# Pooled attention and a feed-forward layer on one core: the first batch times v and the first run in float32 whole, and two pieces for batches 5 to 7

## The chip, the cores and the metric

One core of a Trainium2 chip runs one program. The metric is the device time of one execution in microseconds (us). The kernel before takes 1009.37 us (median of 3 runs, 1008.57 to 1009.87).

## The reference

```python
k_p = k.reshape(B, H, Sp, 8, D).mean(axis=3)      # q, k, v: 8 x 8 x 576 x 64, Sp = 72
v_p = v.reshape(B, H, Sp, 8, D).mean(axis=3)
scores = np.matmul(q, k_p.transpose(0, 1, 3, 2)) / 8
attn = softmax(scores)                             # over the 72 pooled keys
x = heads_side_by_side(np.matmul(attn, v_p))       # 4608 tokens x 512
h = x @ w_in                                       # 512 x 2048
out = np.maximum(0.01 * h, h) @ w_out              # 2048 x 512
```

All inputs and the output are float32.

## The kernel before

**Numbers.** A float32 value that goes into a large matmul is kept as two tiles of the packed type float32r, its rounded value (hi) and the rest (lo). A product is then three matmuls: hi with hi, hi with lo, lo with hi. Splitting a tile costs a cast on ACT and a subtraction on DVE. The scores and all transposes run on float32 as it is; in the trace a float32 matmul is two records.

**Attention.** Keys and values are pooled by POOL (batch 0 in part by DVE). place_k and place_v lay them out: kT by transposes on PE, v_hi and v_lo by a scaled copy on ACT and a subtraction on DVE (L342, L343); the eight keys past 64 go into v_rem through matmuls (pv, L357). A batch has 576 tokens, which PIECES cuts into pieces of one to three tiles. Per tile and group of four heads stand: q transposed (q_unit, pq L369, copied to qT by ACT, L371), scores (s_unit, pss L394, row maximum on DVE, four exponentials e on ACT, L404), division (norm_unit, at, on POOL or DVE, L418), and the transpose of the result (p_unit, pp L443, cast to pT_hi and pT_rem on ACT, pT_lo and pT_rem by DVE, L445 to L453). Per piece and group av_unit makes two accumulators pa of four matmuls each (L468 to L471, at least 256 columns wide except in batch 0), and these are split into x's hi and lo (xh L479, xl L480); tokens past 512 of batches 0 and 1 wait in x_tail (L482).

**Feed-forward.** The 4608 tokens are nine chunks of 512. A part is one chunk with one of 16 blocks f of 128 hidden units: m1 (12 matmuls into ph, L651 to L653), Prelu on ACT (L656), split into gh and gl (L659, L660), and m2 (12 matmuls into four accumulators acc, L675 to L677) two parts later. The table runs orders them: run 0, the first run, is chunk 0 with f 0 to 7; run 1 is chunk 1 whole; run 2 is chunk 0 with f 8 to 15, added to what run 0 left in DRAM (partial); then chunks 2 to 8. A run ends with store (acc copied to o by ACT and DVE, L697, L698, then a DMA).

**Weights.** stage loads them as raw bits; a head (head in convert) turns them into float32 w_t with two activations on ACT (L184, L185) and three operations on DVE (L186, L187, L190), and a tail splits them into w (cast on ACT L194, subtraction on DVE L195). There are 32 of each, spread by convert_to over FIRST (the steps "c"), run 0 and run 1. A head's ACT steps may not be issued ahead of the third last cast of gh (after, with BEHIND). w_t and o share three buffers.

**Order.** PE's order is that in which the code is written. FIRST lists batch 0's units; behind its "/" only two PSUM banks are left for attention, so a transpose or score waits until the bank of two groups back is emptied. Beside each run the attention units of a later chunk are laid between the halves of m1 and m2 by line_up: batch 0's last tile and batch 1 beside run 0, batch 2 on from run 2. The order on ACT, DVE, POOL and SP is found by a scheduler.

## Time and profile before

| | |
|---|---|
| profiled execution | 1009.92 us, of which the span is 1008.1 |
| mean granted clock of PE | 0.978 |
| PE busy | 960.3 us (95%), 4584 instructions |
| PE's weight loads (PEld) | 785.7 us (78%) |
| ACT busy | 427.4 us (42%), 1386 instructions |
| DVE busy | 366.3 us (36%), 890 instructions |
| POOL busy | 177.7 us (18%), 292 instructions |
| DMA | 57.44 MB, mean 57 GB/s |
| chain that ended last | PE 89%, DVE 4%, ACT 3% |
| waits of PE from 59.9 to 134 us | 11.4 us |

Times are of one execution, in us from the start of its span. Matmuls follow each other faster than one lasts (about .23 us from start to start for 512 columns, with a shown duration of .39), so PE's pace is read from the starts. A wait is put down to what ended last before it. Rows of the waits give the total, the times, and the longest; rows of a timeline give start, duration, engine, line, operation and, in brackets, the idle time before and what ended it.

### The profile page before, as it was taken

The numbers are of one execution on the slowest core, as the hardware profiler recorded it, in microseconds if no ns is written. First come the engines' busy times: TensorE is split into PE (matmuls) and PEld (weight loads), VectorE is DVE, ScalarE is ACT, GpSimd is POOL, SyncE is SP. The second block draws the span as 40 slices with busy tenths as digits, with TensorE's granted clock in tenths as the row PEclk, the third lists the DMA queues.
The fourth block names the chain that finished last, engine by engine and source line by source line (L and its number), as shares of the span: only waits on it lengthen the run. The fifth ranks groups of instructions, "written<-read, shape, count | busy, mean of one in ns | idle before, by whom it ended". The sixth has DMA issues, their size and how long they took to land.

```text
span 1008.1 us, 12812 instructions
## 1 busy us (share of the span) xinstructions
PE 960.3 (95%) x4584; PEld 785.7 (78%) x4584; DVE 366.3 (36%) x890; ACT 427.4 (42%) x1386; POOL 177.7 (18%) x292
## 2 busy tenths in 40 slices
PE   4569999999999999999999999999999999999998
PEld 4457778888887878878888788888887788888886
DVE  5998639223333222232222323232322322231111
ACT  4778657234433333434343425333434334332221
POOL 3602200501036510141013301031100001000000
PEclk8689999999999999999999999999999999999999
DMA  9954311302034301130012202020200020001001
GB/s 241 279 172 133 101 46 44 112 23 69 1 107 115 91 8 44 32 92 12 20 44 58 58 11 63 3 61 1 63 11 11 1 63 1 1 1 42 1 1 42
DMA packets 65006, 57.44 MB, mean 57 GB/s; under 512 B 39856, under 2 KB 48048, under 8 KB 64944
## 3 DMA queue, kind: packets, MB, share of 16 engines
q1 hardware_dynamic: 64944, 56.64, 19.8%
q8 instruction: 36, 0.59, 0.2%
q14 instruction: 26, 0.21, 0.1%
HBM read 46.14 MB, written 10.49 MB: 56 GB/s over the span
## 4 chain that ended last, share of the span: by engine, by line
PE 89%; DVE 4%; ACT 3%; issue 1%; DMA 1%; SPq 0%; POOL 0%; DVEq 0%; ACTq 0%; POOLq 0%
PE ph L651 13%; PE acc L675 13%; PE ph L653 13%; PE ph L652 13%; PE acc L677 13%; PE acc L676 13%; PE pss L394 4%; PE pp L443 2%; PE pq L369 2%; ACT e L404 2%; PE pa L468 1%; PE pa L469 1%; PE pa L471 1%; PE pa L470 1%; DVE w_t L187 1%
## 5 line engine op out<-in xcount | busy, mean ns | idle before, releaser
L651 PE MATMUL ph<-xh,w 128*128 128x512 f32 x576 | 236.2, 410 | 0.0
L675 PE MATMUL acc<-w,gh 128*128 128x512 f32 x576 | 234.7, 408 | 0.0
L653 PE MATMUL ph<-xh,w 128*128 128x512 f32 x576 | 227.2, 394 | 0.0
L652 PE MATMUL ph<-xl,w 128*128 128x512 f32 x576 | 227.0, 394 | 0.0
L677 PE MATMUL acc<-w,gl 128*128 128x512 f32 x576 | 225.7, 392 | 0.0
L676 PE MATMUL acc<-w,gh 128*128 128x512 f32 x576 | 225.5, 392 | 0.0
L656 ACT ACTIVATE ph<-ph 128x512 f32<-128x512 f32 x144 | 84.2, 585 | 275.6 <-PE ph L653 275.4
L660 DVE TENSOR_TENSOR gl<-ph,gh 128x512 fp32r<-128x512 f32 x144 | 99.4, 691 | 264.9 <-ACT gh L659 264.0
L418 POOL TENSOR_TENSOR at<-e,red 128x256 f32<-128x256 f32 (+1 forms) x76 | 47.3, 622 | 561.8 <-DVE red L416 428.0
L404 ACT ACTIVATE e<-pss,red 128x72 f32<-128x72 f32 (+1 forms) x320 | 98.0, 321 | 108.8 <-DVE red L402 107.3
L653 PEld LDWEIGHTS ph<-xh,w 128*128 128x128 f32 x576 | 109.3, 190 | 24.4
L677 PEld LDWEIGHTS acc<-w,gl 128*128 128x128 f32 x576 | 108.4, 188 | 24.1
L651 PEld LDWEIGHTS ph<-xh,w 128*128 128x128 f32 x576 | 109.4, 190 | 22.2 <-issue 1.4
L675 PEld LDWEIGHTS acc<-w,gh 128*128 128x128 f32 x576 | 108.4, 188 | 21.9 <-issue 1.9
L652 PEld LDWEIGHTS ph<-xl,w 128*128 128x128 f32 x576 | 109.6, 190 | 19.4
L676 PEld LDWEIGHTS acc<-w,gh 128*128 128x128 f32 x576 | 108.6, 189 | 19.2
L659 ACT CAST gh<-ph 128x512 fp32r<-128x512 f32 x144 | 85.2, 592 | 3.1
L402 DVE TENSOR_REDUCE red<-pss 128x4 f32<-128x288 f32 (+1 forms) x80 | 36.1, 454 | 99.6 <-PE pss L394 98.5
L404 ACT ACTIVATION_READ_ACCUMULATOR e<-pss,red 128x1 f32 (+1 forms) x320 | 65.8, 206 | 0.0
L394 PEld LDWEIGHTS pss<-kT,qT 128*128 128x128 f32 (+1 forms) x320 | 49.4, 192 | 14.7 <-ACT qT L371 5.0
L394 PE MATMUL pss<-kT,qT 128*128 128x144 f32 (+1 forms) x320 | 55.9, 303 | 4.2 <-ACT qT L371 4.2
L449 DVE TENSOR_TENSOR pT_lo<-pp,pT_hi 128x256 fp32r<-128x256 f32 (+1 forms) x80 | 31.6, 395 | 69.5 <-ACT pT_rem L446 68.7
(90 smaller groups left out, 857.3 us busy)
## 6 DMA issues: line engine op xcount, KB each, us to landing
out_dram<-o SPq DMA_DIRECT2D x35, 256.0 KB, 2.1
q<-in_q_dram SPq DMA_DIRECT2D x32, 256.0 KB, 4.2
w_bits<-in_moe_w_in_dram SPq DMA_DIRECT2D x16, 512.0 KB, 3.6
w_bits<-in_moe_w_out_dram SPq DMA_DIRECT2D x16, 512.0 KB, 3.4
k0raw<-in_k_dram SPq DMA_DIRECT2D x16, 256.0 KB, 3.7
k1raw<-in_k_dram SPq DMA_DIRECT2D x16, 256.0 KB, 4.4
v0raw<-in_v_dram SPq DMA_DIRECT2D x16, 256.0 KB, 4.2
v1raw<-in_v_dram SPq DMA_DIRECT2D x16, 256.0 KB, 5.4
```

The lines of the kernel that those rows point to most:

```text
L394: nc.tensor.matmul(sc[:n, 2 * SP * i : 2 * SP * (i + 1)], qT[:, p, :n], kT[:, p, :, :].rearrange("d i s -> d (i s)"), start=True, stop=True,)
L404: ins = nc.scalar.activation(e[:n, h, :], scv[:n, h, :], AF.Exp, bias=mx[:n, h : h + 1], accum_out=sm[:n, h : h + 1],)
L418: eng.tensor_tensor(at[:n, 0:2, :].rearrange("a i (h s) -> a (i h) s", h=2), e[:n, :, 0:MAIN], sm[:n].unsqueeze(2).broadcast_to([n, 4, MAI ...
L651: nc.tensor.matmul(ph, w[:, 0, ks], xh[kk], start=kk == 0, stop=False)
L652: nc.tensor.matmul(ph, w[:, 0, ks], xl[kk], start=False, stop=False)
L653: nc.tensor.matmul(ph, w[:, 1, ks], xh[kk], start=False, stop=kk == NK - 1)
L656: nc.scalar.activation(ph, ph, AF.Prelu, alpha=0.01)
L659: casts.append(nc.scalar.copy(gh, ph))
L660: nc.vector.tensor_tensor(gl, ph, gh.bitcast(F32), op=ALU.subtract)
L675: nc.tensor.matmul(a, gh[:, r], hi, start=first, stop=False)
L676: nc.tensor.matmul(a, gh[:, r], lo, start=False, stop=False)
L677: nc.tensor.matmul(a, gl[:, r], hi, start=False, stop=last)
```

## The change

**Batch 0 times v.** For batch 0, v goes whole into v_first, pT's first two thirds are copied whole to a float32 tile and the rest is scaled on DVE; p·v is two float32 matmuls for an accumulator and not four packed ones (L498, L499 in the changed kernel). v_lo, pT_lo and a cast go.

**The first run.** Batch 0's 512 tokens are kept whole in whole_x (two copies on ACT, two on DVE for a piece; no split). The weights of f 0 to 7 stay as float32 in whole_w. m1 and m2 of run 0 are four float32 matmuls each (L710, L750), Prelu writes g directly (L716), and there is no gh and gl. The splits that runs 1 and 2 need come later: split(f - 3) at part f of run 0, f 5 to 7 in run 1, and chunk 0's x by split_first at f 3 of run 1. Heads are ordered so that w_in is a block ahead of w_out (lagged); their ACT steps, and the casts of the splits, may not be issued ahead of the last activation of m1 that is written before them (paced). FIRST has 3 steps "c" instead of 14, and stage(f + SPARE) is called by the head and not the tail.

**Batches 5 to 7.** They are cut like batches 1 and 4, into 256 and 320 tokens, where there were three pieces each. A piece may now cross the end of a chunk: what is past it is copied by DVE to x_tail or to a tile "over", and carry(c) splits it on ACT and DVE at the start of run c; for c = 2 it takes the place of tails, which stood at the end of run 2.

Lines of the changed kernel stand some 20 to 80 further on: head's ACT steps L206, L207, its DVE steps L208, L209, L212, the split L220, L221, transposes of p L468, xh L520, o L774.

**Moves.** ACT, from the last x copies of batch 0 to the first scores of its last tile, ahead of part 0. Before:

```order
L194 CAST w_1_438<-w_t_439 128x512
L348 ACTIVATE vremparts_829<-vremsum_161 64x64
L479 CAST xh_0_402<-pa_1_0_525 128x256
L479 CAST xh_1_403<-pa_1_1_532 128x256
L194 CAST w_1_493<-w_t_494 128x512
L479 CAST xh_2_404<-pa_1_2_539 128x256
L479 CAST xh_3_405<-pa_1_3_546 128x256
L371 COPY qT_4_564<-pq_4_559 128x4x64
```

And now, where vsum and vremsum are POOL's sums of batch 1:

```order
L517 COPY whole_x_375<-pa_1_0_456 128x256
L369 ACTIVATE v_hi<-vsum_162 64x4x64 x2
L375 ACTIVATE vremparts_696<-vremsum_163 64x64
L517 COPY whole_x_376<-pa_1_2_464 128x256
L398 COPY qT_4_477<-pq_4_472 128x4x64
L431 ACTIVATE e_4_0_493,red_4_0_494<-pss_4_0_490,red_4_0_494 64x72 x4
```

The two casts of weights are gone, and batch 1's v_hi and vremparts stand ahead of the last copy of x.

ACT in part 4 of run 0, around the first x of batch 1. Before:

```order
L404 ACTIVATE e_2_0_983,red_2_0_984<-pss_2_0_980,red_2_0_984 128x72 x4
L656 ACTIVATE ph_4_973<-ph_4_973 128x512
L479 CAST xh_0_1006<-pa_0_0_1001 128x256
L659 CAST gh_4_997<-ph_4_973 128x512
L184 ACTIVATE w_bits_862<-w_bits_862 128x512
L185 ACTIVATE w_bits_862<-w_bits_862 128x512
L479 CAST xh_1_1007<-pa_0_1_1016 128x256
```

And now:

```order
L716 ACTIVATE g_4_839<-ph_4_824 128x512
L206 ACTIVATE w_bits_643<-w_bits_643 128x512
L207 ACTIVATE w_bits_643<-w_bits_643 128x512
L206 ACTIVATE w_bits_595<-w_bits_595 128x512
L207 ACTIVATE w_bits_595<-w_bits_595 128x512
L220 CAST w_2_917<-whole_538 128x512
L220 CAST w_2_920<-whole_538 128x512
L520 CAST xh_0_846<-pa_0_0_841 128x256
L520 CAST xh_1_847<-pa_0_1_856 128x256
```

xh_0 stood directly behind the activation; now two heads and two casts are between.

ACT at the start of run 1, where the first run's accumulators are copied to o. Before:

```order
L656 ACTIVATE ph_1_1438<-ph_1_1438 128x512
L659 CAST gh_1_1452<-ph_1_1438 128x512
L697 COPY o_0_1459<-acc_0_807 128x256
L184 ACTIVATE w_bits_1276<-w_bits_1276 128x512
L185 ACTIVATE w_bits_1276<-w_bits_1276 128x512
L184 ACTIVATE w_bits_1425<-w_bits_1425 128x512
L185 ACTIVATE w_bits_1425<-w_bits_1425 128x512
L697 COPY o_1_1466<-acc_1_811 128x256
L697 COPY o_2_1473<-acc_2_840 128x256
L697 COPY o_3_1480<-acc_3_844 128x256
L656 ACTIVATE ph_2_1504<-ph_2_1504 128x512
```

And now:

```order
L729 ACTIVATE ph_2_1300<-ph_2_1300 128x512
L732 CAST gh_2_1314<-ph_2_1300 128x512
L206 ACTIVATE w_bits_1085<-w_bits_1085 128x512
L774 COPY o_2_1269<-acc_2_707 128x256
L207 ACTIVATE w_bits_1085<-w_bits_1085 128x512
L206 ACTIVATE w_bits_997<-w_bits_997 128x512
L207 ACTIVATE w_bits_997<-w_bits_997 128x512
L549 CAST xh_0_1353<-whole_x_375 128x512
L549 CAST xh_1_1354<-whole_x_375 128x512
L549 CAST xh_2_1355<-whole_x_376 128x512
L549 CAST xh_3_1356<-whole_x_376 128x512
L774 COPY o_3_1274<-acc_3_709 128x256
```

o_2 and o_3 stood ahead of part 2's activation; now they stand behind it, o_3 also behind the four casts of chunk 0's x.

The diff, cut to its core:

```diff
         WHOLE,
-        [[(0, 128), (128, 64)], [(192, 128), (320, 128)], [(448, 128)]],
-        [[(0, 128)], [(128, 128), (256, 128)], [(384, 128), (512, 64)]],
-        [[(0, 64)], [(64, 128), (192, 128)], [(320, 128), (448, 128)]],
+        WHOLE, WHOLE, WHOLE,
...
     FIRST = (
...
-        "c q4 c c / sa40 sa41 sb40 sb41 c c c"
+        "q4 c / sa40 sa41 sb40 sb41"
...
+    WHOLE_W = {0: (1, 0), 1: (2, 0), 2: (3, 0), 3: (6, 0), 4: (6, 1), 5: (7, 0), 6: (7, 1)}
+    whole_w = {}
+    def whole_weights(f):
+        if f not in whole_w:
+            shape, name = [P, 2, DM], f"whole{f}"
+            whole_w[f] = (
+                spare(*WHOLE_W[f], shape, F32, name) if f in WHOLE_W
+                else two.tile(shape, F32, tag="raw", name=name)
+            )
+        return whole_w[f]
+    def paced():
+        after = casts[-1] if casts else anchor.get("act")
+        return tc.issue_after(after.ins) if after else nullcontext()
...
             low, high = b[:, :, 0], b[:, :, 1]
-            ws[i, f] = spare(f, i, [P, 2, DM], F32R, f"w{i}_{f}")
-            t = five.tile([P, DM], I32, tag="o", name=f"w{i}_t{f}")
-            st["w"] = t.bitcast(F32)
-            after = casts[-BEHIND] if len(casts) >= BEHIND else anchor.get("act")
-            with tc.issue_after(after.ins) if after else nullcontext():
+            if f < SPLIT:
+                t = whole_weights(f)[:, i, :]
+                st["w"] = t
+                t = t.bitcast(I32)
+            else:
+                t = five.tile([P, DM], I32, tag="o", name=f"w{i}_t{f}")
+                st["w"] = t.bitcast(F32)
+            with paced():
...
+        def tail():
+            w, t = spare(f, i, [P, 2, DM], F32R, f"w{i}_{f}"), st["w"]
+            ws[i, f] = w
+            with paced() if f < SPLIT else nullcontext():
+                nc.scalar.copy(w[:, 0, :], t)
+            nc.vector.tensor_tensor(w[:, 1, :], t, w[:, 0, :].bitcast(F32), op=ALU.subtract)
...
             r = slice(64 * i, 64 * i + 64)
+            if b == 0:
+                nc.scalar.mul(v_first[r, :, i, :], sums[r], 1.0 / POOL)
+                continue
...
         rem = pc["rem"][:, o : o + n]
+        if b == 0:
+            anchor["act"] = nc.scalar.copy(pc["hi"][:, :, o : o + n], pp[:, 0:2, :n])
+            nc.vector.tensor_scalar_mul(rem, pp[:, 2, :n], m_lo)
+            return
         nc.scalar.copy(pc["hi"][:, :, o : o + n], pp[:, 0:2, :n])
-        ins = nc.scalar.copy(rem, pp[:, 2, :n])
-        if b == 0:
-            anchor["act"] = ins
+        nc.scalar.copy(rem, pp[:, 2, :n])
...
             vr = v_rem[:, g, 2 * i : 2 * i + 2, :].rearrange("a i d -> a (i d)")
-            nc.tensor.matmul(pa, vh, pc["hi"][:, i, :w], start=True, stop=False)
-            nc.tensor.matmul(pa, vh, pc["lo"][:, i, :w], start=False, stop=False)
-            nc.tensor.matmul(pa, vl, pc["hi"][:, i, :w], start=False, stop=False)
-            nc.tensor.matmul(pa, vr, pc["rem"][:, :w], start=False, stop=True)
+            if b == 0:
+                vw = v_first[:, p, :, :].rearrange("a i d -> a (i d)")
+                nc.tensor.matmul(pa, vw, pc["hi"][:, i, :w], start=True, stop=False)
+                nc.tensor.matmul(pa, vr.bitcast(F32), pc["rem"][:, :w], start=False, stop=True)
+            else:
+                nc.tensor.matmul(pa, vh, pc["hi"][:, i, :w], start=True, stop=False)
+                nc.tensor.matmul(pa, vh, pc["lo"][:, i, :w], start=False, stop=False)
+                nc.tensor.matmul(pa, vl, pc["hi"][:, i, :w], start=False, stop=False)
+                nc.tensor.matmul(pa, vr, pc["rem"][:, :w], start=False, stop=True)
...
                 c, o = divmod(2 * TAIL + S * (b - 2) + s0, CH)
-                c, m = c + 2, n
-            if m:
+                c, m = c + 2, min(n, CH - o)
+                if m < n and c + 1 not in waiting:
+                    to = x_tail
+                    if n - m > 2 * TAIL:
+                        to = two.tile([P, NK, POOL * D // 2], F32, tag="raw", name=f"over{c}")
+                    waiting[c + 1] = to, n - m
+            if m and c == 0:
+                (nc.vector.tensor_copy if i else nc.scalar.copy)(whole_x(p)[:, o : o + m], pa[:, :m])
+            elif m:
...
             if m < n:
-                nc.vector.tensor_copy(x_tail[:, p, TAIL * b : TAIL * (b + 1)], pa[:, m:n])
+                to, o = (x_tail, TAIL * b) if b < 2 else (waiting[c + 1][0], 0)
+                nc.vector.tensor_copy(to[:, p, o : o + n - m], pa[:, m:n])
...
+    whole_xs = []
+    def whole_x(kk):
+        if not whole_xs:
+            whole_xs.extend(spare(11, i, [P, 2, CH], F32, f"whole_x{i}") for i in range(2))
+        return whole_xs[kk // 2][:, kk % 2, :]
+    def split_first():
+        for kk, (h, l) in enumerate(zip(*x_parts(0))):
+            with paced():
+                nc.scalar.copy(h, whole_x(kk))
+            nc.vector.tensor_tensor(l, whole_x(kk), h.bitcast(F32), op=ALU.subtract)
+    waiting = {2: (x_tail, 2 * TAIL)}
+    def carry(c):
+        held, n = waiting[c]
+        for kk, (h, l) in enumerate(zip(*x_parts(c))):
+            w = held[:, kk, :n]
+            nc.scalar.copy(h[:, :n], w)
+            nc.vector.tensor_tensor(l[:, :n], w, h[:, :n].bitcast(F32), op=ALU.subtract)
...
         n, c, f = parts[k]
+        nm = f"{c}_{f}"
+        ph = ps_h.tile([P, CH], F32, tag="h", name=f"ph{nm}")
+        if n == 0:
+            for kk in range(NK):
+                ks = slice(kk * P, (kk + 1) * P)
+                nc.tensor.matmul(
+                    ph, whole_w[f][:, 0, ks], whole_x(kk), start=kk == 0, stop=kk == NK - 1
+                )
+                if kk == 1:
+                    yield
+            g = three.tile([P, CH], F32, tag="gh", name=f"g{nm}")
+            casts.append(nc.scalar.activation(g, ph, AF.Prelu, alpha=0.01))
+            gs[k] = g, None
+            yield
+            return
...
         w = ws[0, f]
-        nm = f"{c}_{f}"
-        ph = ps_h.tile([P, CH], F32, tag="h", name=f"ph{nm}")
...
         gh, gl = gs.pop(k)
-        hi, lo = ws[1, f][:, 0, :], ws[1, f][:, 1, :]
+        if n > 0:
+            hi, lo = ws[1, f][:, 0, :], ws[1, f][:, 1, :]
...
             a = accs[t]
-            nc.tensor.matmul(a, gh[:, r], hi, start=first, stop=False)
-            nc.tensor.matmul(a, gh[:, r], lo, start=False, stop=False)
-            nc.tensor.matmul(a, gl[:, r], hi, start=False, stop=last)
+            if n == 0:
+                nc.tensor.matmul(a, gh[:, r], whole_w[f][:, 1, :], start=first, stop=last)
+            else:
+                nc.tensor.matmul(a, gh[:, r], hi, start=first, stop=False)
+                nc.tensor.matmul(a, gh[:, r], lo, start=False, stop=False)
+                nc.tensor.matmul(a, gl[:, r], hi, start=False, stop=last)
...
-    for i, f in [(i, f) for f in range(NF) for i in range(2)]:
+    def lagged(lo, hi):
+        fs = [(0, f) for f in range(lo, hi)], [(1, f) for f in range(lo, hi)]
+        out = [fs[0].pop(0)]
+        while fs[1]:
+            out += [side.pop(0) for side in fs if side]
+        return out
+    steps, splits, last = [], {}, None
+    for i, f in lagged(0, SPLIT):
+        head, splits[i, f] = convert(i, f)
+        steps.append(head)
+    for i, f in lagged(SPLIT, NF):
         head, tail = convert(i, f)
-        steps.append(head)
-        if last:
-            steps.append(last)
+        steps += [head, last] if last else [head]
...
+    def split(f):
+        for i in range(2):
+            if (i, f) in splits:
+                splits.pop((i, f))()
...
         us = list(units[n])
+        if n >= 2 and n in waiting:
+            us.insert(0, lambda n=n: carry(n))
...
             if n == 0:
-                convert_to(14 + 2.8 * f)
+                convert_to(3 + 2 * (f + 1) + max(0, f - 5))
+                split(f - 3)
             elif n == 1:
-                convert_to(36 + 3 * f)
+                split(f + SPLIT - 3)
+                convert_to(2 * SPLIT + 4 + 3 * (f + 1))
+                if f == 3:
+                    split_first()
```

More of the change, by code (lines that the diff above doesn't have):

```diff
@@ L60, in tile_pooled_attention_ffn @@
         WHOLE,
[3 rows of a table removed]
+        WHOLE, WHOLE, WHOLE,
     ]
     FIRST = (
[3 rows of a table removed]
+        "lk ku q0 q1 sa00 sb00 sa01 sb01 lv sa10 sb10 sa11 sb11 q2 sa20 sa21 vu pu00 pu10 sb20 q3 "
+        "pu01 pu11 sb21 au00 sa30 sa31 c au01 pu20 pu21 sb30 sb31 c pu30 pu31 au10 au11 "
+        "q4 c / sa40 sa41 sb40 sb41"
     )
@@ L120, in tile_pooled_attention_ffn @@
     nc.gpsimd.memset(kT, 0.0)
+    nc.gpsimd.memset(v_first, 0.0)
     nc.gpsimd.memset(v_hi.bitcast(F32), 0.0)
@@ L190, in head @@
             nc.vector.tensor_tensor(t, t, low, op=ALU.add)
-        def tail():
-            w, t = ws[i, f], st["w"]
-            nc.scalar.copy(w[:, 0, :], t)
-            nc.vector.tensor_tensor(w[:, 1, :], t, w[:, 0, :].bitcast(F32), op=ALU.subtract)
             if i == 1:
                 stage(f + SPARE)
+        def tail():
[4 more added lines that the diff above has]
+            nc.vector.tensor_tensor(w[:, 1, :], t, w[:, 0, :].bitcast(F32), op=ALU.subtract)
         return head, tail
@@ L372, in q_unit @@
         return qT
-    WIDE = {("at", 1): (8, 0), ("at", 2): (8, 1), ("at", 3): (7, 0),
-            ("e", 1): (7, 1), ("e", 2): (6, 0), ("e", 3): (6, 1)}
+    WIDE = {("at", 1): (0, 0), ("at", 2): (0, 1), ("at", 3): (1, 1),
+            ("e", 1): (2, 1), ("e", 2): (3, 1), ("e", 3): (8, 0)}
     wides = {}
@@ L431, in piece_tiles @@
     def piece_tiles(b, j, g):
-        if b > 0 or g == 0 or j == 2:
+        if b > 0:
             return pT
-        return {
-            part: spare(10 - n // 2, n % 2, t.shape, F32R, f"pT_{part}{b}_{j}_{g}")
-            for n, (part, t) in enumerate(pT.items())
-        }
+        t = spare(10 - j % 2, g, [P, 3, PMAX], F32, f"pT{b}_{j}_{g}")
+        return {"hi": t[:, 0:2, :], "rem": t[:, 2, :]}
     def p_unit(b, t, g, at, pc, o):
@@ L494, in x_parts @@
         return xs[c]
-    def tails():
-        for kk, (h, l) in enumerate(zip(*x_parts(2))):
-            h, l = h[:, : 2 * TAIL], l[:, : 2 * TAIL]
-            nc.scalar.copy(h, x_tail[:, kk, :])
-            nc.vector.tensor_tensor(l, x_tail[:, kk, :], h.bitcast(F32), op=ALU.subtract)
+    whole_xs = []
[15 more added lines that the diff above has]
+            nc.vector.tensor_tensor(l[:, :n], w, h[:, :n].bitcast(F32), op=ALU.subtract)
     q_of = {}
@@ L708, in store @@
             nc.sync.dma_start(out[r : r + P, :], o)
-    steps = []
-    last = None
-    for i, f in [(i, f) for f in range(NF) for i in range(2)]:
+    def lagged(lo, hi):
[9 more added lines that the diff above has]
+    for i, f in lagged(SPLIT, NF):
         head, tail = convert(i, f)
-        steps.append(head)
-        if last:
-            steps.append(last)
+        steps += [head, last] if last else [head]
         last = tail
@@ L762, in tile_pooled_attention_ffn @@
         if n == 2:
-            us = [fetch] + us + [tails]
+            us = [fetch] + us
         units.append(us)
```

2 lines of the change are left out of this document (1 added, 1 removed), and 2 rows, old and new, of the table FIRST.

## Prediction

> **What bounds the kernel now.** I read the page's slices first, then the windows of the opening stages, the waits of PE from 59.9 us until run 1, and last the timelines of PE, ACT and DVE at single places. The sum is made against the profiled execution (1009.92 us: a span of 1008.1 and 1.8 around it); the median of the runs shown is 1009.37, so .55 comes off at the end. The 40 slices of 25.2 us, in tenths:
>
> ```profile
> PE   4569999999999999999999999999999999999998
> PEclk8689999999999999999999999999999999999999
> ```
>
> From the sixth slice on PE is full, at full clock; time is lost in the first five. Later the kernel gets shorter only through fewer PE columns, or longer through a new wait. The windows: PE, PEld, DVE, ACT and POOL busy (with counts), granted clock, DMA share, GB/s:
>
> ```profile
> 40.00:50.00 10.00, 5.69 (x23) 4.67 (x24) 10.00 (x26) 6.97 (x19) 3.69 (x7) 0.50 0.92 293
> 60.00:134.00 74.00, 62.58 (x308) 49.70 (x307) 54.34 (x134) 55.40 (x176) 11.36 (x20) 0.93 0.39 116
> 112.00:114.00 2.00, 2.00 (x5) 1.53 (x5) 1.08 (x3) 0.81 (x2) 0.75 (x2) 0.50 0.68 245
> 210.00:220.00 10.00, 10.00 (x46) 8.29 (x45) 2.07 (x6) 3.33 (x8) 0.00 (x0) 1.00 0.01 2
> ```
>
> Before the first run DVE is the bound (10.00 of 10). Beside it nobody is: DVE 73%, ACT 75%, PE 85%, and PE's clock is .93. There single waits decide. Steady runs (210 to 220) have ACT and DVE free two thirds of the time. PE's waits from 59.9 to 134 (total, times, longest):
>
> ```profile
> PE pp L443 <- DVE x_tail L482: 3.1, 2, 1.8
> PE pq L369 <- ACT e L404: 2.6, 2, 2.1
> PE pq L369 <- DVE kT L330: 2.4, 1, 2.4
> PE pa L469 <- DVE pT_lo L449: 0.9, 1, 0.9
> ```
>
> These make 9.0; seven smaller rows bring it to 11.4. Nearly all are one kind: the next transposes or scores wait for their PSUM bank (two are left after the "/") to be emptied by ACT or DVE, which have weight work queued ahead.
>
> **The change, part by part.** PE's timeline at the places that I use (start, duration, idle before):
>
> ```profile
> 51.94 0.50 PE L651 MATMUL ph<-xh,w 128*128 128x512 f32 x1
> 56.52 0.72 PE L443 MATMUL pp<-ident,at 64*128 64x64 f32 x3 [2.92 <-POOL at L418]
> 59.90 0.26 PE L468 MATMUL pa<-pT_hi,v_hi 128*128 128x64 f32 x1
> 111.21 0.57 PE L369 MATMUL pq<-ident,q 64*128 64x64 f32 x4 [2.08 <-ACT e L404]
> 133.94 0.39 PE L651 MATMUL ph<-xh,w 128*128 128x512 f32 x1
> ...
> 61.40 0.28 PE L468 MATMUL pa<-pT_hi,v_hi 128*128 128x64 f32 x1
> 61.52 0.28 PE L469 MATMUL pa<-pT_lo,v_hi 128*128 128x64 f32 x1
> ```
>
> Part 0 runs from 51.94 to 59.90; run 1 begins at 133.94.
>
> *The start.* Eleven weight steps and batch 0's splits leave ACT and DVE ahead of part 0. What is late next is POOL, with batch 1's v sums, since ACT's v_hi and vremparts of batch 1 now stand ahead of its last whole_x copy (the first order excerpt). POOL's last sums, and ACT's two steps as they ran elsewhere:
>
> ```profile
> 42.60 0.63 POOL L235 TENSOR_TENSOR vsum<-v1raw 128x128 f32<-128x128 f32 x1
> 43.20 0.49 POOL L235 TENSOR_TENSOR vremsum<-vremraw 64x64 f32<-64x64 f32 x1
> ...
> 20.17 0.90 ACT L342 ACTIVATE v_hi<-vsum 64x256 fp32r<-64x256 f32 x2
> 47.70 0.25 ACT L348 ACTIVATE vremparts<-vremsum 64x64 fp32r<-64x64 f32 x1
> ```
>
> vsum is there at 43.2; .9 for v_hi, .25 for vremparts, some .3 for the copy: 44.7, then qT_4 and scores: part 0 begins at about 45 if POOL keeps its times. It takes 3.4 us of float32 matmuls (below) and 2 of units and hops, since the 2.92 us wait for POOL at 56.52 has gone by then (batch 0's last pieces are normalized while PE waits for x). So part 0 ends at 50.4 and not 59.90: **-9.5**. If POOL stays behind, 4 of these are lost.
>
> *Float32 in the first run.* Prices, from scores (two float32 matmuls of 144 columns, four records) beside packed matmuls:
>
> ```profile
> 89.20 0.65 PE L394 MATMUL pss<-kT,qT 128*128 128x144 f32 x4
> 89.59 0.49 PE L675 MATMUL acc<-w,gh 128*128 128x512 f32 x1
> 89.92 0.39 PE L676 MATMUL acc<-w,gh 128*128 128x512 f32 x1
> 90.15 0.39 PE L677 MATMUL acc<-w,gl 128*128 128x512 f32 x1
> ...
> 100.76 0.28 PE L468 MATMUL pa<-pT_hi,v_hi 128*128 128x256 f32 x1
> 101.71 0.39 PE L651 MATMUL ph<-xh,w 128*128 128x512 f32 x1
> ...
> 124.93 0.31 PE L468 MATMUL pa<-pT_hi,v_hi 128*128 128x320 f32 x1
> 126.10 0.39 PE L675 MATMUL acc<-w,gh 128*128 128x512 f32 x1
> ```
>
> A packed 512 column matmul lasts .227 (89.92 to 90.15, rounded). The scores hold PE for .39, and the next packed matmul then stands .10 longer than .23 (89.59 to 89.92): .49 for 288 columns, or .87 for 512 in proportion, .85 with a fixed start taken off; I take .857. A half part (m1 or m2) is 4 x .857 = 3.43 instead of 12 x .227 = 2.72: +.71. Thirteen half parts lie between part 0 and run 1: **+9.2**. If the .10 is not the scores' own but a price of the change of format, a matmul costs .39/288 x 512 = .69, a half part 2.77, and the term is +.7; the .10 would then also go at most of the 42 changes in this stage (4.2 us). I lean to the first reading, and take half of the 4.2 back: **-2.1**. The two m2 of the first run that fall into run 1: **+1.4**. The 64 token piece of batch 0: 16 matmuls of .12 (61.40 to 61.52) become 8 at about the same: **-.9**.
>
> *The first run's waits.* ACT's and DVE's weight work, from their timelines:
>
> ```profile
> 61.62 0.69 ACT L184 ACTIVATE w_bits<-w_bits 128x512 f32<-128x512 f32 x1
> 63.83 0.61 ACT L194 CAST w<-w_t 128x512 fp32r<-128x512 f32 x1
> 64.34 0.27 ACT L445 CAST pT_hi<-pp 128x128 fp32r<-128x128 f32 x1
> ...
> 59.50 0.69 DVE L187 SCALAR_TENSOR_TENSOR w_t<-w_bits,w_t 128x512 int32<-128x512 int32 x1
> 60.10 0.69 DVE L195 TENSOR_TENSOR w<-w_t,w 128x512 fp32r<-128x512 f32 x1
> ```
>
> Two heads take ACT 2.2 us (61.62 to 63.83), a cast .51, a long DVE step .6. The change takes an activation's second pass and gl away, but sets two heads directly behind each activation, and from part 3 on two casts and two subtractions (second excerpt). In part 4, xh_0 stands behind g_4, two heads and two casts: .5 + 2.2 + 1.0. xl_0 stands behind DVE's six head steps and two subtractions (4.3) that begin 1.1 after the activation's input: 5.4, + .4 for itself, + .2 to reach PE. Until then pp_0_1 has no bank; PE has .9 of p·v to do: 5.1, and .2 for the hand-over between the two heads: 5.3. In part 1 to 2, kT stands behind four head activations on ACT and five head steps on DVE, and pq_0 waits for its bank: 3.9, where the 2.4 now was. By the same count: pq_4 behind e_3_0 2.7, batch 0's last p·v 1.05, pv behind v_rem and the two subtractions 1.6 and 1.0, the end of the run 1.7, one of .3. Together 17.5 against 11.4: **+6.2**. Bounds: half of today's (5.7), if the heads always find a gap; 20, if the hops add up.
>
> *The clock.* A clock of .93 over 74 us is 5.2 us lost. The 2.08 us wait at 111.21 is followed by 112 to 114 at .50 (1 us lost, .3 or more outside the window). Three waits longer than that, at some 1.5 each, make 4.5: **-.7**. The Trainium skill ("TensorE: Matmul & The Clock Gate", "Part 1: The HAM clock gate") states that the clock is halved after an idle window of about 3.4 us. By that rule pq_4's wait of 2.7 would cost no slow clock and the sum would be 1.5 us less; the .50 behind a 2.08 us gap speaks against it here, so I keep the row.
>
> Up to run 1's first matmul: -9.5 + 9.2 - 2.1 - .9 + 6.2 - .7 = +2.2; it begins near 136.
>
> *Run 1's entry.* ACT now, where the first run's accumulators are emptied:
>
> ```profile
> 143.39 0.38 ACT L697 COPY o<-acc 128x256 f32<-128x256 f32 x1
> 144.78 0.65 ACT L184 ACTIVATE w_bits<-w_bits 128x512 f32<-128x512 f32 x1
> 145.33 0.64 ACT L185 ACTIVATE w_bits<-w_bits 128x512 int32<-128x512 uint32 x1
> 145.87 0.63 ACT L697 COPY o<-acc 128x256 f32<-128x256 f32 x2
> 146.66 0.37 ACT L697 COPY o<-acc 128x256 f32<-128x256 f32 x1 [0.16 <-DMA partial<-o]
> ```
>
> These copies stand ahead of ph_2, and PE has no wait. In the changed kernel (third excerpt) o_2 stands behind ph_2, gh_2 and one activation (.5 + .5 + .56, + .3 for itself), o_3 behind three more (1.66) and four x casts of .51: 5.8 after m1 of part 2 ends, and DVE's halves likewise behind gl_2 and four subtractions. acc_2's first matmul is due 1.4 after that end, acc_3's 2.0: waits of 1.0 and, from there, 5.0: **+6.0**. What hides it if I am wrong is a gap in which ACT runs ahead; it is in order, so I see none.
>
> *Batches 5 to 7.* Three pieces are 48 p·v matmuls of 256 columns per batch (shorter ones are padded); two are 16 of 256 and 16 of 320. By the rows, .119 (eight in .95) and .146 (eight in 1.17): 5.7 becomes 4.2, three times: **-4.4**. The overflow copies and carry(c) go to ACT and DVE, busy 3.33 and 2.07 of 10 there, so I cost them at nothing; without that cover each boundary costs some 1.5. The waits of p·v from 110 on are small already:
>
> ```profile
> PE pa L468 <- ACT e L404: 0.9, 3, 0.5
> ```
>
> Sum: +2.2 + 1.4 + 6.0 - 4.4 = +5.2, so 1015.1, less .55: **1014.5 us**.
>
> **Rivals.** *R1, faster.* The first run's waits fall to half of today's, 5.7 for 17.5: -11.8, 1002.7. For it: a quarter less DVE and ACT work beside the first run, and ACT at 75% already leaves gaps; against it: both engines are in order, and the heads stand directly ahead of what PE waits for. It decides from the point where these waits total 12.3, break-even. *R2, no change.* The wait at run 1's entry doesn't show because acc_3's copy gets through: -6.0, 1008.5. For it: the copies cost nothing today; against it: the four casts ahead of o_3. *R3, the late pieces give nothing*, because the wider p·v waits for two or three p transposes at a time, or carry stands in front of an activation: +4.4, 1019.0. Against it: the .9 us above for all such waits, and batches 1 and 4 are already cut so.
>
> **How the numbers follow.** Forecast .46, R1 .30, R2 .14, R3 .10. The forecast's own range is 1010.5 to 1018.5 (waits 13.5 to 20, the start 4 less or the format price 4 more given back). The whole range takes in most of R1 and R3: 1002.0 to 1020.0. A measurement tells .2%, 2.0 us, from no change. Faster is R1, .30; same is R2, .14; slower is the forecast and R3, .56.
>
> **What would show it.** Right: the first activation of part 0 near 49 and run 1's first matmul near 136; L710 and L750 with four 512 column float32 matmuls in 3.4 us; PE waits of some 17 before run 1, the longest at pp_0_1 and pq_0; acc's first matmul waiting for o in run 1's third part, about 5; batches 5 to 7 1.5 us shorter each. Wrong: run 1 before 130 (R1), no wait for o (R2), or part 0 still past 50 because POOL is late.

## The result and the profile after

The changed kernel takes 1026.95 us (median of 4 runs, 1025.86 to 1027.68) against 1009.62 for the kernel before: a ratio of 1.016, 95% interval 1.0139 to 1.0181. That is 1.6% slower: the forecast had the direction, but the loss is 17.3 us and not 5, and the time lies outside the range. The profiled execution took 1027.68 us, with a span of 1025.9. Its slices of 25.6 us, answering to those of before:

```profile
PE   5767897999999999999999999999999999999998
...
PEclk8898898999999999999999999999999999999999
```

PE is fuller in the first two slices, and has holes, with a clock below full speed, up to the seventh. The windows of the stretch ahead of the first run, of the first run behind part 0, of a place in it and one at run 1's entry, and of a steady run (columns as before):

```profile
40.00:50.00 10.00, 8.19 (x30) 5.52 (x30) 7.36 (x18) 4.46 (x21) 2.45 (x5) 0.80 0.59 172
52.96:145.66 92.70, 74.97 (x255) 40.94 (x255) 54.72 (x133) 52.24 (x169) 10.94 (x20) 0.89 0.36 110
118.00:126.00 8.00, 6.63 (x14) 3.65 (x15) 4.82 (x11) 3.41 (x16) 1.35 (x2) 0.57 0.73 226
165.00:180.00 15.00, 10.53 (x38) 8.55 (x39) 12.86 (x23) 7.65 (x15) 0.00 (x0) 0.77 0.20 66
210.00:220.00 10.00, 10.00 (x46) 8.29 (x45) 0.69 (x1) 1.17 (x2) 5.54 (x8) 1.00 0.41 105
```

The second row is the reading that the prediction missed: a granted clock of .89 for 92.7 us, where the kernel before had .93 for 74.0. The waits of PE in that window, and the one in run 1's entry:

```profile
PE pp L468 <- DVE xl L521: 5.3, 1, 5.3
PE pq L396 <- DVE kT L354: 3.8, 1, 3.8
PE pq L396 <- ACT e L431: 2.6, 1, 2.6
PE pv L384 <- ACT qT L398: 1.9, 1, 1.9
PE pp L468 <- DVE x_tail L524: 1.5, 2, 1.3
PE pa L499 <- DVE pT L473: 1.2, 1, 1.2
PE pv L384 <- ACT e L431: 0.8, 1, 0.8
...
PE acc L752 <- DVE o L775: 6.2, 2, 4.5
```

With two rows of .4 and .2 the waits of the first run make 17.7; 17.5 was predicted, with 5.3, 3.9 and 2.7 for the three longest, and 6.0 for the last row.

The half clock comes in steps. In all the traces of this case the granted clock changes only on a grid of 3.41 us, and between the first loads and the last matmul each slow stretch lasts one step or several whole ones. Those of the changed kernel behind part 0, and then those of the kernel before in its first run (PE busy stands behind the window's length, the clock behind POOL's column):

```profile
64.53:67.94 3.41, 2.87 (x7) 1.84 (x8) 1.26 (x4) 0.59 (x1) 0.00 (x0) 0.50 0.64 181
78.19:81.60 3.41, 3.41 (x6) 1.33 (x5) 0.24 (x2) 0.00 (x0) 0.97 (x2) 0.50 0.50 159
98.66:105.49 6.83, 5.10 (x11) 2.92 (x12) 2.69 (x7) 0.59 (x3) 0.00 (x0) 0.50 0.50 154
119.14:125.97 6.83, 6.60 (x14) 3.65 (x15) 3.68 (x9) 2.24 (x9) 1.35 (x2) 0.50 0.70 212
166.93:173.75 6.82, 4.28 (x10) 3.41 (x11) 6.79 (x13) 2.13 (x5) 0.00 (x0) 0.50 0.11 42
```

```profile
63.62:67.03 3.41, 3.41 (x12) 2.83 (x11) 2.53 (x7) 3.40 (x8) 0.00 (x0) 0.50 0.31 118
73.87:77.27 3.40, 3.40 (x12) 2.82 (x11) 3.31 (x8) 0.55 (x4) 0.00 (x0) 0.50 0.81 223
111.41:114.81 3.40, 3.40 (x12) 2.70 (x11) 1.58 (x5) 1.25 (x3) 0.97 (x2) 0.50 0.80 230
```

A slow stretch costs half of the time in which PE is busy in it: 1.7 us for one step and up to 3.4 for two, less what lies in the wait itself.

PE's timeline at the turning points:

```profile
47.84 1.98 PE L710 MATMUL ph<-whole_x,whole 128*128 128x512 f32 x4
52.96 0.43 PE L498 MATMUL pa<-pT,v_first 128*128 128x64 f32 x2
...
89.98 1.88 PE L710 MATMUL ph<-whole_x,whole 128*128 128x512 f32 x4
91.70 0.65 PE L421 MATMUL pss<-kT,qT 128*128 128x144 f32 x4
92.19 1.88 PE L710 MATMUL ph<-whole_x,whole 128*128 128x512 f32 x4
...
145.66 0.39 PE L724 MATMUL ph<-xh,w 128*128 128x512 f32 x1
```

Part 0 begins at 47.84 (51.94 before) and ends at 52.96 (59.90). Two float32 matmuls last 1.72 (89.98 to 91.70), one .86. The scores hold PE for .49 with float32 behind them as well (91.70 to 92.19), so the .10 that was in doubt is the scores' own. Run 1 begins at 145.66 (133.94).

Counted by the starts of the parts in both traces, the changed kernel is 6.9 us ahead at the end of part 0, 11.7 behind at run 1's start, 22.0 behind at part 4 of run 1 (177.72 against 155.70), still 22.1 behind in the middle (513.06 against 490.95 at run 5) and 17.8 at the end (1020.74 against 1002.98). A second trace of the changed kernel (e14_again) has part 0 at 47.3 and run 1 at 146.5.

### The profile page after: what moved, and what is told of

Same layout as the page of the kernel before. It is cut to its first block, busy times and chain, and to the rows that moved or that the text cites. A ratio compares the mean times of both kernels' runs of the same rounds, so it can differ in the third digit from the quotient of the medians.

```text
span 1025.9 us, 12585 instructions
## 1 busy us (share of the span) xinstructions
PE 972.2 (95%) x4472; PEld 770.3 (75%) x4472; DVE 362.8 (35%) x882; ACT 423.1 (41%) x1368; POOL 176.5 (17%) x293
## 4 chain that ended last, share of the span: by engine, by line
PE 88%; ACT 4%; DVE 3%; DMA 2%; SPq 2%; issue 1%; ACTq 0%; DVEq 0%
PE ph L724 12%; PE acc L752 12%; PE ph L726 12%; PE ph L725 12%; PE acc L754 12%; PE acc L753 12%; PE pss L421 4%; PE pp L468 2%; PE ph L710 2%; PE acc L750 2%; PE pq L396 2%; ACT e L431 1%; SPq L265 1%; DMA kremraw<-in_k_dram 1%; PE pa L502 1%
## 5 line engine op out<-in xcount | busy, mean ns | idle before, releaser
L752 PE MATMUL acc<-w,gh 128*128 128x512 f32 x544 | 220.2, 405 | 6.2 <-DVE o L775 6.2
L724 PE MATMUL ph<-xh,w 128*128 128x512 f32 x544 | 222.3, 409 | 0.0
L726 PE MATMUL ph<-xh,w 128*128 128x512 f32 x544 | 213.3, 392 | 0.0
L725 PE MATMUL ph<-xl,w 128*128 128x512 f32 x544 | 213.0, 392 | 0.0
L754 PE MATMUL acc<-w,gl 128*128 128x512 f32 x544 | 212.9, 391 | 0.0
L753 PE MATMUL acc<-w,gh 128*128 128x512 f32 x544 | 212.7, 391 | 0.0
L733 DVE TENSOR_TENSOR gl<-ph,gh 128x512 fp32r<-128x512 f32 x136 | 93.9, 690 | 260.6 <-ACT gh L732 259.9
L729 ACT ACTIVATE ph<-ph 128x512 f32<-128x512 f32 x136 | 79.5, 584 | 249.0 <-PE ph L726 249.0
L752 PEld LDWEIGHTS acc<-w,gh 128*128 128x128 f32 x544 | 102.3, 188 | 27.9 <-DVE o L775 7.1
L726 PEld LDWEIGHTS ph<-xh,w 128*128 128x128 f32 x544 | 102.4, 188 | 22.7
L754 PEld LDWEIGHTS acc<-w,gl 128*128 128x128 f32 x544 | 102.3, 188 | 22.6
L724 PEld LDWEIGHTS ph<-xh,w 128*128 128x128 f32 x544 | 102.7, 189 | 20.8 <-issue 1.2
L725 PEld LDWEIGHTS ph<-xl,w 128*128 128x128 f32 x544 | 102.8, 189 | 18.7 <-issue 0.5
L753 PEld LDWEIGHTS acc<-w,gh 128*128 128x128 f32 x544 | 102.5, 188 | 18.6
```

Source lines behind the costliest of these rows:

```text
L724: nc.tensor.matmul(ph, w[:, 0, ks], xh[kk], start=kk == 0, stop=False)
L725: nc.tensor.matmul(ph, w[:, 0, ks], xl[kk], start=False, stop=False)
L726: nc.tensor.matmul(ph, w[:, 1, ks], xh[kk], start=False, stop=kk == NK - 1)
L729: nc.scalar.activation(ph, ph, AF.Prelu, alpha=0.01)
L733: nc.vector.tensor_tensor(gl, ph, gh.bitcast(F32), op=ALU.subtract)
L752: nc.tensor.matmul(a, gh[:, r], hi, start=first, stop=False)
```

## The experiments

Theory A: the loss over the forecast lies in what follows PE's waits. Each wait behind conversion work that ACT and DVE have queued costs its length, and then a stretch at half clock. Theory B: the float32 matmuls hold the clock down themselves, whatever the waits. Ratios are to the kernel before on the same chip, with 95% intervals.

**The two parts apart.** e1_pieces is the kernel before with the pieces and carry alone, e2_first the changed kernel with the three pieces for batches 5 to 7:

```diff
 # e1_pieces, on the kernel before
-        [[(0, 128), (128, 64)], [(192, 128), (320, 128)], [(448, 128)]],
...
+        WHOLE, WHOLE, WHOLE,
 # with waiting, carry and the overflow copies as in the change
```

> The kernel before with the second part of the change alone: batches 5 to 7 in pieces of 256 and 320 tokens over chunk ends, with carry. The trace of the changed kernel shows run 3 to the end 4.3 us shorter. If the two parts are independent: 4 us faster than before, some 1005.5, with the first run and run 1 as in the kernel before. If the late gain needed what the first part does to the queues: no change, 1009.5.

> The changed kernel with the three pieces per batch of before for batches 5 to 7, so the first part of the change alone. If the parts are independent: 1031, that is 21 to 22 us slower than before, with run 1 over some 22 us late and nothing given back later. If the late pieces had cost something that the first part hid: less than 1027.

e1_pieces: 1007.67 us, .9974 (.9961 to .9987). From run 4 to the end its trace gains 4.35 us (389.78 to 1000.26 against 388.14 to 1002.98), as much as the changed kernel's. It had started that stretch 1.6 late (part 0 itself 2.2 late, where both kernels have the same order), so by time it is 2.6 us faster and not 4. e2_first: 1032.74, 1.022 (1.0192 to 1.0248); its trace, of the fastest of its executions (1028.06), is 18 to 20 us late from run 1's part 4 on and gives nothing back. Within these intervals the parts are independent; the loss is the first part's.

**The entry of run 1.** e3_xsplit_late:

```diff
-                if f == 3:
+                if f == 6:
                     split_first()
```

> The changed kernel with split_first called at f 6 of run 1 instead of f 3; the four casts and subtractions of chunk 0's x then stand behind o_3's copies on ACT and DVE. Theory A (the loss is waits of PE behind queued conversion work, and a halved clock behind each): the two waits of acc for o at run 1's entry, 6.2 us, fall to about 2.7 since gh_2, gl_2 and the head activations stay ahead, and the slow stretch from 165 to 180 (granted clock .77, 3.4 us lost) mostly goes: 4 to 6.5 us faster than the changed kernel, 1020.5 to 1023. Theory B (float32 matmuls lower the clock by themselves, and the casts would only wait elsewhere): at most 1 us faster, 1026.

1024.03 us, 1.0135 (1.0118 to 1.0151): about 3 us off the changed kernel. The wait row of the entry:

```profile
PE acc L752 <- DVE o L775: 2.6, 2, 1.7
```

2.6 where 2.7 was worked out. From run 1's start to its part 4 the trace is 4.2 us shorter than that of the changed kernel. The casts in front of o_3 made most of the 4.5 us wait, and the slow stretch behind it fell from 6.83 to 3.41 us. By the trace theory A has the gain at its lower end, by time just below it.

**Filling the waits.** If a halved clock follows idle PE, PE should be faster with more to do. e4_fill adds matmuls by zero ahead of the long waits:

```diff
+    FILL = {"q0": 4, "vu": 2, "pu01": 6, "q4": 3, "pu21": 1}
...
+                nc.tensor.matmul(accs[t], zero, whole_x(0), start=False, stop=False)
...
+            if n == 1 and first and t >= 2:
+                fill({2: 2, 3: 5}[t])
```

> The changed kernel with 23 more float32 matmuls of 512 columns by an all-zero weight, added to an accumulator (the result stays the same; the first four go to a bank that nobody reads), put on PE directly ahead of its longest waits: 4 ahead of pq_0, 2 ahead of pv, 6 ahead of pp_0_1, 3 ahead of pq_4, 1 ahead of pp_2_1, 2 and 5 ahead of the two waits for o in run 1. At full clock they are 19.7 us of work and about as long as the waits (3.8, 2.7, 5.3, 2.6, 1.3, 6.2). Theory A: PE has work through the waits, the granted clock in the first run rises from .89 to about .97 and at run 1's entry from .77 to 1, and the kernel becomes 6 to 10 us faster, 1017 to 1021, though it does 19.7 us more work. Theory B: the clock stays near .89, the added work costs what it cannot hide, and the kernel is 0 to 8 us slower, 1027 to 1035.

1023.10 us, 1.0122 (1.0104 to 1.014): 4 us faster with 19.7 us more work, less than expected. The trace shows why: part 0 began at 53.5 and not at 47.8, and the first loads were slower (169 to 182 GB/s from 14 to 20 us in the kernels that have one more small tile, against 258 to 289 in the others). e15_fill64 repeats it with a tile of 64 bytes, and e17_pad4 is the control, the changed kernel with an idle tile of 4 bytes:

```diff
+    zero1 = const.tile([P, 16], F32, name="zero")    # e15_fill64; [P, 1] in e4_fill
...
+    pad = const.tile([P, 1], F32, name="pad")        # e17_pad4, never read
```

> The changed kernel with the same 23 matmuls by zero ahead of the waits as in e4_fill, but the zero tile is 64 bytes long per partition instead of 4. In the four kernels with a further 4 byte tile the loads of the first 40 us moved 172 to 174 GB/s from 14 to 20 us instead of 267 to 281, and part 0 began some 5 us late. If that is the placement of the tiles behind the 4 bytes: the loads are as fast as in the changed kernel, part 0 begins at 47 to 51, run 1 at 136 to 140, and the time is 1016 to 1020, the whole of the 6 to 10 us that theory A gives the clock. If the fill itself delays the start, or a later start was made good anyway: 1022 to 1024 as in e4_fill.

> The changed kernel with one further tile of 4 bytes per partition ahead of the others, set to zero and never used. If the 4 bytes slow the loads: 170 to 180 GB/s from 14 to 20 us, POOL's first sum of batch 1 some 4 us later than 26.8, part 0 at 51 to 54; the time then tells what a late start costs the changed kernel, 1027 (made good by waits) to 1032. If not: 267 to 281 GB/s and 1027.

e15_fill64: 1021.70, 1.0124 (1.0101 to 1.0147). e17_pad4: 1029.25, 1.0184 (1.0163 to 1.0206). The 64 bytes didn't help (part 0 at 50.8), so it is not the 4 bytes. Against the control with the same slow loads, the fill is worth 6 us by the ratios and 7.5 by the medians (the control's four executions spread from 1025.8 to 1031.6); run 1 begins at 141.5 against 149.0, 1.7 of it through an earlier part 0. The windows of e15_fill64, first run and entry:

```profile
54.00:142.00 88.00, 84.20 (x294) 44.15 (x294) 57.09 (x137) 54.35 (x174) 13.85 (x22) 0.98 0.38 116
160.00:180.00 20.00, 19.73 (x78) 14.35 (x77) 17.14 (x31) 12.60 (x24) 0.00 (x0) 1.00 0.19 60
```

The clock goes from .89 to .98 and at the entry from .77 to 1.00, with all the float32 matmuls in place and more of them. Theory B falls. Theory A's 6 to 10 us hold against the control, near their lower end, and not against the changed kernel itself.

**What one gap costs.** e11_gaps makes gaps on purpose in steady packed runs:

```diff
+            nc.scalar.mul(junk, gh[:, 0:1].bitcast(F32), 0.0)
+            for _ in range(GAPS[f]):                  # {4: 2, 7: 6, 10: 11, 13: 18}
+                nc.scalar.mul(junk, junk, 0.0)
+            for _ in range(1 if n == 4 else 8):
+                nc.tensor.matmul(
+                    accs[0], junk.broadcast_to([P, P]), xh[0].bitcast(F32), start=False, stop=False
+                )
```

> The kernel before with eight gaps of PE made on purpose in steady runs whose clock is 1.00: in runs 4 and 5, at the parts with f 4, 7, 10 and 13, a chain of 3, 7, 12 and 19 one-column ACT steps hangs on gh, and PE waits for its end (some 1.5, 2.3, 3.5 and 5 us) before matmuls by an all-zero weight (result unchanged): one of them in run 4, with packed matmuls behind, eight in run 5, so that 7 us of float32 stand behind each gap. Theory A: a gap of about 2 us or more is followed by half clock for 3 to 4 us, whichever format follows, so the loss behind a gap is 1.5 to 2 us in both runs. Theory B: packed matmuls bring the clock back within 2 us or never lose it, and float32 behind the gap stays at half clock for 6 us or more.

Three-microsecond windows behind the gaps of 2.0 (run 4, then run 5) and of 2.9 us (run 4, then run 5) (behind POOL's column stand the clock, the DMA share and GB/s):

```profile
421.60:424.60 3.00, 2.93 (x6) 1.87 (x7) 0.04 (x1) 0.02 (x1) 0.00 (x0) 0.61 0.00 0
553.20:556.20 3.00, 3.00 (x7) 1.43 (x8) 0.00 (x0) 0.00 (x0) 0.00 (x0) 1.00 0.00 0
447.10:450.10 3.00, 2.98 (x5) 1.76 (x6) 0.00 (x0) 0.00 (x0) 0.24 (x1) 0.50 0.00 0
450.10:453.10 3.00, 3.00 (x8) 2.33 (x8) 0.00 (x0) 0.00 (x0) 0.00 (x0) 0.52 0.00 0
583.60:586.60 3.00, 2.97 (x4) 1.42 (x5) 0.00 (x0) 0.00 (x0) 2.11 (x3) 0.50 0.46 114
586.60:589.60 3.00, 3.00 (x4) 1.10 (x4) 0.00 (x0) 0.00 (x0) 0.81 (x1) 0.51 0.29 61
589.60:592.60 3.00, 3.00 (x8) 1.33 (x7) 0.00 (x0) 0.00 (x0) 1.18 (x2) 1.00 0.00 0
```

Behind 2.9 us of idle PE six microseconds run at half clock, 3 us lost, in packed and in float32 work alike. Behind 2.0 us it happened once (1.9 us lost) and once not. By the starts of the parts against the kernel before (less the gap, and .86 for each added matmul), the gaps of 4.1 and 5.7 us cost 2.7 and 2.4 in packed work, those of 5.9 and 5.7 us 1.8 each in float32. So a longer gap costs less, not more. The slow stretch behind all six gaps of 2.9 us or more is two steps of 3.41 us, and it begins while PE still waits; in a longer gap more of it has passed when PE starts again. The stretches of the packed gaps of 2.9, 4.1 and 5.7 us, where PE is busy for 5.88, 5.16 and 4.49 us:

```profile
446.18:453.00 6.82, 5.88 (x12) 3.99 (x13) 0.00 (x0) 0.79 (x4) 1.08 (x2) 0.50 0.00 0
473.48:480.30 6.82, 5.16 (x12) 3.65 (x13) 0.67 (x3) 2.74 (x15) 0.00 (x0) 0.50 0.01 2
500.79:507.61 6.82, 4.49 (x9) 2.88 (x10) 0.00 (x0) 2.00 (x10) 0.00 (x0) 0.50 0.00 0
```

The seven gaps that cost anything cost 2.4 us on average, more than the 1.5 to 2 that theory A had. This is one execution, of 1092.35 us.

**The pacing.** e6_behind3 undoes one line of the change:

```diff
-        after = casts[-1] if casts else anchor.get("act")
+        after = casts[-3] if len(casts) >= 3 else anchor.get("act")
```

> The changed kernel with the old pacing: ACT's steps of heads and of the held back splits may be issued behind the third last activation of m1 and not only behind the last. In the order on ACT the heads run ahead where ACT is free, chunk 0's x casts come before part 1's activation of run 1, and o_2 and o_3 again stand ahead of part 2's activation. Theory A (waits behind queued conversion work, and the clock behind them): the waits of acc for o (6.2 us) and the slow stretch behind them (3.4) are gone, kT's and xh_0's waits get shorter by 1 to 3: 9 to 14 us faster than the changed kernel, 1013 to 1018. Theory B (float32 by itself): at most 3 us faster, 1024 to 1027.

1017.29 us, 1.0065 (1.0041 to 1.009): some 9.5 us of the 17.3 come back, as theory A had it. The window of run 1's entry, and the longest waits of the first run:

```profile
145.00:180.00 35.00, 35.00 (x141) 26.31 (x141) 26.33 (x49) 25.70 (x49) 0.00 (x0) 1.00 0.24 76
```

```profile
PE pq L396 <- DVE kT L354: 4.6, 1, 4.6
PE pa L501 <- ACT e L431: 3.5, 1, 3.5
```

At the entry PE has no wait left and full clock, as o_2 and o_3 again stand ahead of part 2's activation. In the first run kT's wait got longer (4.6 for 3.8), and pp_0_1's 5.3 gave way to 3.5 at another place; run 1 begins 3.4 earlier.

e13_behind3_fill fills what is left there ("q0": 5, "vu": 2, "au00": 4, "q2": 1):

> The changed kernel with the old pacing, and 12 matmuls by an all-zero weight (10.3 us, result unchanged) ahead of the waits that are left there: 5 ahead of pq_0 (4.6 us), 2 ahead of pv (2.6), 4 ahead of the first p times v of batch 1 (3.6), 1 ahead of pq_2. A wait of 2 us or more costs some 2.4 us of halved clock behind it, by the gaps made on purpose; three such waits here, so 5 to 7 us of the 8.2 that the clock of .89 from 60 to 135 us costs come back: 1011 to 1014. If the clock is not what the waits cost (theory B), or ACT and DVE only make PE wait longer once it is faster: 1016 to 1018. Below 1009: float32 was hidden altogether.

1018.14 us, 1.0081 (1.0064 to 1.0098). Part 0 began at 52.4 instead of 47.1, again with a small tile more; from there to run 1 it is 4.5 us shorter (90.7 against 95.2), at a clock of 1.00 from 60 to 143 us. The gain in the run and the loss at the start cancel, so the expectation missed, and the time alone decides nothing.

**DVE's queue.** e9_pool_sub moves the held back subtractions to POOL, e12_pool_behind3 adds the old pacing:

```diff
+            eng = nc.gpsimd if f < 5 else nc.vector
+            eng.tensor_tensor(w[:, 1, :], t, w[:, 0, :].bitcast(F32), op=ALU.subtract)
```

> The changed kernel with the subtractions of the held back weight splits of f 0 to 4 on POOL (busy 10.9 of 92.7 us there) and not on DVE: ten steps of .6 leave DVE's queue in the first run. By the count that gave 5.3 for pp_0_1, DVE then reaches xl_0 1.2 earlier, but xl_0 waits for ACT's xh_0 from there: 3.8. Theory A: that wait falls to about 3.8, run 1 begins 1.5 to 3 us earlier, 1024 to 1025.5. Rival: POOL's steps hold up DVE's by as much as they take off, no change, 1027.

> The changed kernel with both the old pacing (behind the third last activation) and the subtractions of splits f 0 to 4 on POOL. Theory A: the first run's waits fall below those of the old pacing alone, 1013 to 1016. What then remains over the kernel before is the price of float32 (10.7 us of PE work) less the start and the late pieces. If it comes near 1010 or below, the waits were all of the loss and float32 was hidden; if it stays at 1017, POOL gives nothing.

e9_pool_sub: 1026.52, 1.0174 (1.0146 to 1.0202), no change; e12_pool_behind3: 1022.23, 1.0112 (1.0081 to 1.0142), no better than the old pacing alone (its trace is of its fastest execution, 1016.93). In e9_pool_sub pp_0_1's wait was 5.1 and not 3.8. The trace shows why. The last head step ahead of xl_0 on DVE, first in the changed kernel and then in e9_pool_sub, and POOL's two subtractions:

```profile
99.33 0.68 DVE L212 CUSTOM_DVE_ANT_0 whole<-w_bits,whole 128x1024 uint16<-128x1024 uint16 x1
...
100.09 1.53 DVE L212 CUSTOM_DVE_ANT_0 whole<-w_bits,whole 128x1024 uint16<-128x1024 uint16 x1
99.41 3.35 POOL L222 TENSOR_TENSOR w<-whole,w 128x512 fp32r<-128x512 f32 x2 [1.54 <-ACT w L220]
```

While POOL subtracted, DVE's step took 1.53 us for .68, so most of the 1.3 us that left DVE's queue came back. That is the rival of the expectation. Why the two slow each other isn't shown here.

**PE's work against the waits.** e5_half_m1 leaves out half of m1 in the first run:

```diff
-            for kk in range(NK):
+            for kk in (0, 2):
```

> The changed kernel with two of the four float32 matmuls of each m1 of the first run left out (the sum over the 512 inputs takes only the first and third quarter in these eight parts, so the output is not the reference's). That removes 16 matmuls of .857, 13.7 us of PE work, and nothing on ACT or DVE. If PE's work and its waits simply add up in the first run (theory A as the prediction summed it): run 1 begins some 13 us earlier, 1014. If the first run is bound by the loops over ACT and DVE, so that PE only arrives earlier and waits longer: half of it or less comes through, 1020 to 1025.

1019.16 us, 1.0094 (1.0071 to 1.0117): 8 us come through of 13.7, just past the second expectation (half or less). Two waits of its first run that the changed kernel didn't have, or had shorter:

```profile
PE pa L501 <- ACT e L431: 3.1, 1, 3.1
PE pp L468 <- POOL at L445: 1.5, 1, 1.5
```

PE arrives earlier and waits more. Work and waits in this stage add up only in part.

**In the packed first run.** e7_start adds to e1_pieces batch 0's p·v in float32; e8_fill_packed and e16_fill64_packed add matmuls by zero ("pu40": 3, "q0": 2, "q4": 2, "pu21": 2), with a tile of 4 and of 64 bytes:

> The kernel before with the two-piece batches 5 to 7 and, of the first part of the change, batch 0's p times v alone in float32 (v_first, two matmuls for four, no pT_lo and v_lo of batch 0); the first run stays packed, with the old pacing. DVE loses about 4 us and ACT about 3 us of work in the stretch ahead of part 0, where DVE and ACT bound the kernel. If that work sets the start: part 0 ends some 3 us earlier, 1004.5 against 1007.7 for the pieces alone. If the start of the changed kernel came from the held back weight work alone: no difference to the pieces alone, 1007.5.

> The kernel before with the two-piece batches 5 to 7, and 9 matmuls by an all-zero weight (7.7 us, result unchanged) ahead of four of PE's waits in the packed first run: 3 ahead of batch 0's last transposes (2.9 us wait), 2 ahead of pq_0 (2.4), 2 ahead of pq_4 (2.1), 2 ahead of pp_2_1 (1.8). Theory A: the clock is halved behind waits whatever the format, so the granted clock from 60 to 134 us rises from .93 to about .97 and the time falls by 2 to 4 us against the pieces alone, 1004 to 1006. Theory B: packed matmuls lose nothing to waits, the added work costs 0 to 3 us, 1008 to 1010.

> The kernel before with the two-piece batches 5 to 7 and the 9 matmuls by zero of e8_fill_packed, with the zero tile 64 bytes long. If the 4 bytes cost e8_fill_packed its start: 1004 to 1006.5, 1 to 4 us faster than the pieces alone (1007.7). If the packed first run gains nothing from a full clock since ACT and DVE set its pace: 1007 to 1009.

e7_start: 1007.02, .9971 (.9957 to .9985), no difference to the pieces alone. Part 0 began at 54.2 as in e1_pieces (54.1), so the earlier start of the changed kernel comes from the work that is held back (the weights' and, which this run does not separate, batch 0's x splits), not from p·v. e8_fill_packed: 1010.19, 1.0005 (.9993 to 1.0017); e16_fill64_packed: 1012.34, 1.0009 (.9997 to 1.0022). Both are slower than the pieces alone, against theory A's number: the clock from 60 to 135 us rose from .91 to .95 in e16_fill64_packed, but its first run lasted 84.3 us against 81.0, with kT's wait at 3.1 behind the two matmuls put ahead of it. Part 0 also began 1.4 to 2 us later than in e1_pieces, and no run here has the packed kernel with an idle tile, so how much of the loss is the fill's is not shown.

**The changed kernel once more.**

> The changed kernel itself once more, for a second trace and a time beside the others on this chip. Part 0 of the first run began at 47.8 us in its first trace, and between 47.1 and 53.5 in five kernels that have the same work ahead of it; 51.9 to 56.1 in four kernels that have that of the kernel before. If the start gains some 5 us and not the 6.9 between the two first traces: part 0 at 47 to 51 and run 1 at 142 to 146, 1026 to 1028.

1026.79 us, 1.0169 (1.0147 to 1.019). In this trace ACT's v_hi of batch 1 waited 3.66 us for POOL's sum, the bound that the prediction named; in the first trace POOL was done by 42.3, and PE's own chain set part 0.

## Why the prediction was wrong

- **The start** (-9.5): 6.9 in the two first traces. POOL kept its times, but batch 0's own p·v ran late and at half clock (.80 from 40 to 50 us). Part 0 lasted 5.1, where 5.4 was worked out.
- **Float32** (+9.2, +1.4): .86 a matmul, as taken. **The format price** (-2.1) was wrong: nothing came back, and the first reading should have been taken whole.
- **The waits** (+6.2): 17.7 against 11.4, +6.3; place and length of the three longest were right.
- **The clock** (-.7): this is the step that failed. "Three waits longer than that, at some 1.5 each, make 4.5": there were four places, and up to 3.4 us at each. Behind the wait of 3.8 and behind that of 1.9 (with .8 close after it) came one slow step each, behind those of 5.3 and 2.6 two each. That is 10.2 us by the clock, and 9.0 in which PE worked (half of the 17.98 busy in the first four rows above), so the term is +3.8 over the 5.2 of before. The stretch behind the wait of 2.08 us, read as 1 us "and .3 or more outside the window", lasts from 111.41 to 114.81 and cost 1.7; and one of the three stretches of before stands behind waits of .9 and 1.25 us close together, which the count of long waits leaves out. The size is not a fixed one: in five traces with the same longest waits to .2 us, half clock behind part 0 of the first run lost 5.1 (e2_first, e9_pool_sub), 8.5 (e17_pad4), 10.2 (the changed kernel) and 12.0 us (e14_again). The rule of the Trainium skill that was weighed there ("TensorE: Matmul & The Clock Gate", "Part 1: The HAM clock gate", an idle window of about 3.4 us) would have gone further off: the 2.6 us wait of pq_4 was followed by .57 from 118 to 126, and gaps of 2.9 us halved the clock twice of two.
- **Run 1's entry** (+6.0): the waits were 6.2, but the sum behind the 6.0 does not hold as written: if o_3 is free 5.8 after m1 and acc_3 is due 2.0 after it, the waits make 3.8. The rest is DVE's half, which the prediction names and doesn't add up. PE went on at 169.47, when that was done, so the right number is partly luck. The clock behind the waits had no term: 3.4 us (.23 of 15), of which 2.1 while PE worked. Without the 1.4 the entry cost 8.9. The two copies of o_3:

```profile
167.07 0.37 ACT L774 COPY o<-acc 128x256 f32<-128x256 f32 x1
169.00 0.42 DVE L775 COPY o<-acc 128x256 f32<-128x256 f32 x1
```

- **Batches 5 to 7** (-4.4): 4.3 gained in the changed kernel's trace, 4.35 alone.

The misses of the start (2.6), the format price (2.1), the clock (4.5) and the entry's clock (2.1) make 11.3, and the small ones .4 more; between the 17.8 of the two profiled spans and the 5.2 of the sum lie 12.6. So about 1 us has no place. R1 and R2 were wrong in their waits, R3 in the pieces; R1's ground, a quarter less work beside the first run, did not hold either (DVE busy 54.7 us for 54.4, ACT 52.2 for 55.4).

What stays open: why one more small tile ahead of the others goes with slower first loads, why the same wait is followed by one slow step in one execution and by two or none in another, why POOL's subtractions lengthen DVE's steps, and how much of the start is PE's chain and how much POOL, which changes from one execution to the next. The best version run here is the second part of the change alone, e1_pieces (e7_start is the same within the intervals).
